# Block 1's first pair of token tiles: seven products in place of eight, in a linear-attention block gated by a mixer

## The chip, the core and the metric

One NeuronCore of a Trainium2 chip runs the whole kernel. The time is what the device needs for one execution, in microseconds (us); several executions are timed and their median is given. A profiled execution comes with a trace: for every instruction its engine, its start, its length and what it waited for. The engines are TensorE (PE, with the loading of its stationary operand shown apart as PEld), VectorE (DVE), ScalarE (ACT), GpSimd (POOL) and SyncE (SP), which issues most DMAs. POOL issues the DMAs that add to what lies at their destination.

## What is computed

2048 tokens of 512 features go through a layer norm, then two branches, whose product is added to the input:

```python
def _A_ref(x, wqkv, wo):                 # linear attention, 32 heads of 16
    q, k, v = ...                        # x @ wqkv, by heads
    phi = lambda t: jnp.where(t > 0, t + 1, jnp.exp(t)) + 1e-6
    pq, pk = phi(q), phi(k)
    kv = jnp.einsum("bhsd,bhse->bhde", pk, v)
    z = jnp.einsum("bhsd->bhd", pk)
    num = jnp.einsum("bhqd,bhde->bhqe", pq, kv)
    den = jnp.einsum("bhqd,bhd->bhq", pq, z)[..., None] + 1e-6
    return (num / den) ... @ wo
...
xn = _layernorm(x)
s = _A_ref(xn, A_wqkv, A_wo)
g = _silu(_B_ref(xn, B_w1, B_w2, B_w3, B_w4))
return x + s * g
```

`_B_ref` is a token mixer (shifts by one and two tokens between two 512 x 512 products) and a channel MLP of width 1376. For this change only the keys and queries matter: phi(x @ Wk) and phi(x @ Wq) for every token.

## The kernel before

**Tiling.** The tokens are cut into 16 tiles of 128, numbered 0 to 15, and four blocks of four tiles (block 1 is tiles 4 to 7). The 512 features are four chunks of 128. Every fp32 operand of a product is split into an upper half (rounded to the matmul format, by ScalarE) and a lower half (the rest, by VectorE's subtraction), and a product is three matmuls: upper x upper, upper x lower, lower x upper (`products`, L495). So a key tile, four chunks into 512 columns, is 12 matmuls (`project`, L707).

**Keys and queries one by one.** `key` (L783) and `query` (L806) make one tile each in one PSUM bank. In blocks 1 to 3 ScalarE copies the bank out with the token's scale (`zi`, `qi`). Then `phi_k` (L904) or `phi_q` (L915) applies phi: an exponential on ScalarE, a minimum and maximum on VectorE. For a key come two halves (`k4h`, `k4l` and so on) for the gram and a gather that adds it into `zacc`; for a query a store to memory (`pqd`).

**Keys and queries by pairs.** `pair_kq(i)` (L870) makes the keys and queries of tiles i and i+2 together. It sees them as a 2 x 2 block product, tokens (i, i+2) and feature halves against feature halves and (key, query), and forms the four results from seven products instead of eight, in Winograd's form of Strassen's method. A product covers two chunks, so it is six matmuls and a pair is 42, where four single results are 48. The products go into three banks: `pax`, `pbx`, which accumulates four of the seven with copies taken out between them, and `pex`. ScalarE copies four times (`p1x`, `p5x`, `u2x`, `zk`), VectorE joins three times (`zi`, `qi`, `qk`).

The seven products need sums of the weights (`kq_t1` to `kq_t4`, made once by `forms_w`, L820) and sums of tokens (`forms_x`, L844): eight additions on VectorE (`xf`), then four roundings on ScalarE and four lower halves on VectorE (`xs_0h`, `xs_0l` to `xs_3l`). The second argument `j0` of `forms_x` is the first pair of the block for which the sums are made: with 0 their width is 256 tokens (both pairs), with 1 it is 128 (the second pair alone).

Before the change, blocks 2 and 3 used `pair_kq` for both of their pairs. Block 1 made tiles 4 and 6 by `key` and `query` and only tiles 5 and 7 as a pair; its sums were made by `forms_x(1, 1)`. Block 0 uses single tiles throughout. [...]

**What a block's tokens wait for.** The transposed tokens are loaded (`xt`), and a gather adds each token's negative mean from a row in memory (`nrow`). That row comes from the tile statistics, by POOL, a small transpose on PE (`ab`), a copy (`ar`) and a store (`spread`, L631). ScalarE and VectorE then make the halves `u_0` to `u_3`, one per chunk (`load_u`, L660).

**Order.** The program is first written as a list of operations. `Plan.emit` (L285) then decides the order on each engine. It works through its own estimates of durations and picks, among operations whose inputs are there, the one that is due first. PE's due times follow the order of the list; those of the other engines are worked back from PE's. PE may run ahead of its list within a window of 9 us by these estimates, and free PSUM banks and pool tiles limit it. A table, `SOONER`, moves single operations: a pair (n, k) makes operation n due 0.25 k us earlier, or later for negative k. The order written into the program is fixed; on the chip only waits remain.

Of the kernel before, what the change touches and what calls it, by code (L numbers as in the profile page):

```python
# [411 lines left out]
def linear_attn_gated_by_mixer(  # L412
# [1224 lines left out]
    forms_x(1, 1)  # L1637
# [9 lines left out]
    for b in range(1, NQ):  # L1647
        t0 = b * QT
        if b > 1:
            pair_kq(t0)  # L1650
        else:
            for i in (t0, t0 + 2):
                key(i)
                query(i)
        if b > 1:
            gram(t0 - 3)
            gram(t0 - 1)
        if b < NQ - 1:
            for j in range(QT):
                load_rows(t0 + QT + j)  # L1660
            spread(b + 1)
            load_u(b + 1, 1)
            scale_x(t0 + QT, QT)
            forms_x(b + 1)
        if b == 3:
            sums_w4(1)
        pair_kq(t0 + 1)
        if b == NQ - 1:
            W1 = Weights("w1", w1)
            W1.split()  # L1670
        gram(t0)
        gram(t0 + 2)
        if b == 2:
            sums_w4(0)
        if b == 3:
            sums_w4(2)
# [37 lines left out]
    b = 2  # L1714
# [24 lines left out]
    b = 3  # L1739
# [29 lines left out]
    for b in range(NQ):  # L1769
# [35 lines left out]
        for j in range(QT):  # L1805
            i = b * QT + j
# [7 lines left out]
    for b in LINE:  # L1814
# [119 lines left out]
```

## Time and profile before

| | |
|---|---|
| median of three runs | 499.14 us (498.49 to 500.01) |
| profiled execution, its own time | 499.65 us |
| its span, first to last instruction | 497.9 us |
| granted TensorE clock | 1.00 |
| instructions | 9898, of them 3244 matmuls |
| DMA | 117.44 MB, mean 236 GB/s |
| POOL, busy | 121.5 us, 24% of the span |

In lines of the timeline stand the start (us from the span's start), the length (us), the engine, the line of the kernel, and the operation as output<-inputs; brackets hold how long the engine was idle before it and what ended that. Lines of a tile give a count and minimum, median and maximum in ns. Since most operations go through a few helpers, one line (L146 for matmuls, L168 for ScalarE, L191 and L201 for VectorE) stands for many; the tile's name tells them apart. Buffer numbers are left out of the names, so `xs_0l` stands for that sum in all blocks.

### The profile page before, as it was taken

To read this page: it belongs to the slowest core of one execution; us is meant where nothing else is said; L and a number is where in the kernel's file an instruction comes from. 1 tells how busy PE (TensorE), PEld (TensorE's weight loads), DVE (VectorE), ACT (ScalarE), POOL (GpSimd) and SP (SyncE) were. 2 spreads that over 40 slices of the span, in tenths; PEclk is the share of its full clock that TensorE was granted. 3 is DMA by queue.
4 is the path that set the end of the run, shared out by engine and by line. 5 is a ranking of instruction groups with operands and counts; after the bars stand their busy time and mean duration, and the time that the engine had idled before them with its cause. 6 is when DMAs were issued, how large, how long until landed. Compare 5 with 4: busy or idle time off the path is not lost.

```text
span 497.9 us, 9898 instructions
## 1 busy us (share of the span) xinstructions
PE 492.0 (99%) x3244; PEld 446.9 (90%) x3244; DVE 438.2 (88%) x874; ACT 373.9 (75%) x845; POOL 121.5 (24%) x214
## 2 busy tenths in 40 slices
PE   9999999999999999999999999999999999999996
PEld 6678877888888989899899999999999999999996
DVE  5898987789989759999999999999999789796964
ACT  5999999667787589999987667865686686655531
POOL 1384413357930223133100021100000000143420
PEclk9999999999999999999999999999999999999999
DMA  7869596999983899989986699884543799589996
GB/s 236 293 187 278 136 286 208 207 298 267 337 230 97 209 299 275 283 230 282 361 276 188 208 189 289 239 276 141 170 127 111 239 319 318 152 185 306 275 252 175
DMA packets 87083, 117.44 MB, mean 236 GB/s; under 512 B 10328, under 2 KB 39160, under 8 KB 87032
## 3 DMA queue, kind: packets, MB, share of 16 engines
q1 hardware_dynamic: 75512, 96.11, 59.2%
q0 software_dynamic: 11520, 20.71, 24.5%
q8 instruction: 25, 0.41, 0.3%
q14 instruction: 26, 0.21, 0.2%
HBM read 72.66 MB, written 39.93 MB: 226 GB/s over the span
## 4 chain that ended last, share of the span: by engine, by line
PE 62%; issue 4%; DMA 2%; ACT 1%; POOL 0%; DVE 0%; POOLq 0%; ACTq 0%
PE pb L146 11%; PE pbd L146 9%; PE acc L146 6%; PE pe L146 6%; PE ped L146 5%; PE pbs L146 5%; PE pbm L146 3%; PE pa L146 3%; PE pad L146 3%; PE pes L146 2%; DMA o<-xnd 2%; PE a L146 2%; PE h L146 2%; PE pem L146 2%; PE pas L146 1%
## 5 line engine op out<-in xcount | busy, mean ns | idle before, releaser
L225 POOL DMA_DIRECT2D xo<-x1d x12 | 11.2, 950 | 165.6 <-ACT d_s10h L168 111.1
L225 POOL DMA_DIRECT2D o<-xnd x16 | 14.0, 884 | 39.7 <-DVE o L191 24.9
L225 POOL DMA_DIRECT2D th<-in_x x14 | 12.3, 878 | 45.3 <-DVE th L201 13.0
L225 POOL DMA_DIRECT2D zacc<-ke x12 | 13.5, 1125 | 28.1 <-DVE u_2l L191 8.7
L168 ACT ACTIVATE th<-xo 128x512 f32<-128x512 f32 (+1 forms) x16 | 9.6, 612 | 13.6 <-DVE xo L201 9.8
L225 POOL DMA_DIRECT2D xt<-nrow x16 | 14.6, 1281 | 7.4 <-DVE kq_t31l L191 3.1
L191 DVE TENSOR_TENSOR ht<-h,abc 128x512 f32<-128x512 f32 x16 | 11.0, 687 | 5.0 <-PE h L146 4.9
L168 ACT ACTIVATE u<-pb 128x256 f32<-128x256 f32 x20 | 7.6, 382 | 7.4 <-PE pb L146 7.1
L196 POOL TENSOR_SCALAR w<-mv 128x4 f32<-128x4 f32 (+2 forms) x10 | 2.7, 269 | 41.2 <-ACT sq L168 40.9
L168 ACT ACTIVATE y<-o,nm,rs 128x512 f32<-128x512 f32 x16 | 12.0, 806 | 0.2 <-DVE wo_2l L191 0.2
L168 ACT ACTIVATE sq<-o,mv 128x512 f32<-128x512 f32 x16 | 11.4, 717 | 0.1
L201 DVE SCALAR_TENSOR_TENSOR pq<-pq,rd 128x512 f32<-128x512 f32 x16 | 10.8, 682 | 0.3
L201 DVE SCALAR_TENSOR_TENSOR qz<-pq,zb 128x512 f32<-128x512 f32 x16 | 10.9, 682 | 0.0
L168 ACT ACTIVATE p<-pe 128x256 f32<-128x256 f32 x20 | 7.7, 383 | 4.3 <-PE pe L146 3.7
L168 ACT ACTIVATE ht<-ht 128x512 f32<-128x512 f32 x16 | 9.9, 624 | 1.3 <-DVE ht L191 1.2
L1471 DVE TENSOR_REDUCE den<-qz 128x32 f32<-128x512 f32 x16 | 10.7, 677 | 0.1
L168 ACT ACTIVATE sq<-o 128x512 f32<-128x512 f32 x16 | 10.0, 623 | 1.0 <-DMA o<-xnd 1.0
L168 ACT ACTIVATE p<-pb 128x256 f32<-128x256 f32 x20 | 7.7, 384 | 3.6 <-PE pb L146 3.2
L613 POOL TENSOR_TENSOR rs<-w,nhalf 128x4 f32<-128x4 f32 (+2 forms) x10 | 9.4, 941 | 0.8
L201 DVE SCALAR_TENSOR_TENSOR th<-th,so 128x512 f32<-128x512 f32 x12 | 8.2, 682 | 1.1 <-ACT th L168 1.0
L168 ACT ACTIVATE x<-x,nm,rs 128x512 f32<-128x512 f32 x12 | 9.1, 802 | 0.0
L168 ACT ACTIVATE sq<-x,mv 128x512 f32<-128x512 f32 x12 | 8.6, 718 | 0.1
(2075 smaller groups left out, 2442.1 us busy)
## 6 DMA issues: line engine op xcount, KB each, us to landing
w_s<-in_w SPq DMA_DIRECT2D x28, 256.0 KB, 6.6
x<-in_x SPq DMA_DIRECT2D x16, 256.0 KB, 5.3
xt<-in_xt SPq DMA_DIRECT2D x16, 256.0 KB, 6.7
xnd<-x SPq DMA_DIRECT2D x16, 256.0 KB, 7.0
xt<-nrow POOLq DMA_DIRECT2D x16, 256.0 KB, 7.2
pqd<-qr SPq DMA_DIRECT2D x16, 256.0 KB, 5.6
o<-xnd POOLq DMA_DIRECT2D x16, 256.0 KB, 6.9
x1d<-o SPq DMA_DIRECT2D x16, 256.0 KB, 6.0
```

The source lines that it names most:

```text
L146: lambda: nc.tensor.matmul(out.get(), lhs.get(), rhs.get(), start=start, stop=stop, skip_group_check=more))
L168: nc.scalar.activation(out.get(), src.get(), func, scale=get(scale), **kw)
L191: self.vec(eng, out, [a, b], lambda: self.e(eng).tensor_tensor(out.get(), a.get(), b.get(), op=op), True)
L196: lambda: self.e(eng).tensor_scalar(out.get(), a.get(), get(s1), get(s2), **kw), False,
L201: lambda: self.nc.vector.scalar_tensor_tensor(out.get(), a.get(), get(s), b.get(), op0=op0, op1=op1),
L225: lambda: self.nc.gpsimd.dma_start(out.get(), get(src), accum_op=ALU.add), mb=mb)
L613: lambda: g.tensor_tensor(out.get(), src.get(), nh.get(), op=ALU.pow))
L1471: pl.add("DVE", .6, .68, [t], [den], lambda: nc.vector.tensor_reduce(den.get(), t.get().rearrange("p (h d) -> p h d", d=DH), axis=AX.X, op ...
```

## The change

`pair_kq` now makes block 1's first pair too (tiles 4 and 6), and the sums of block 1's tokens are made at double width, for both of its pairs. The table `SOONER` is another one: the list of operations is different from there on, so its numbers no longer mean the same operations, and it was searched again. Its entries reach over the whole kernel, so the order of any engine may differ anywhere.

```diff
     scale_x(QT, QT)
-    forms_x(1, 1)
+    forms_x(1, 0)
     spread(0)
...
     for b in range(1, NQ):
         t0 = b * QT
-        if b > 1:
-            pair_kq(t0)
-        else:
-            for i in (t0, t0 + 2):
-                key(i)
-                query(i)
+        pair_kq(t0)
         if b > 1:
             gram(t0 - 3)
...
     SOONER = (
-        48, -110, 56, 31, 58, 1, 65, 7, 88, -136, 91, -34, 100, 23, 101, 2, 106, -95, 119, 3, 121, -105, 124, 8,
...
+        21, 58, 25, 16, 26, -109, 34, 16, 37, 2, 42, 7, 48, 40, 65, 14, 74, 5, 79, -34, 82, -111, 88, -2, 91,
...
     )
```

127 rows, old and new, of the table SOONER are left out of this document.

## The prediction

> **What bounds the kernel now.** I read the page first: its busy times, then its chain of work that ended last.
>
> ```profile
> span 497.9 us, 9898 instructions
> PE 492.0 (99%) x3244; PEld 446.9 (90%) x3244; DVE 438.2 (88%) x874; ACT 373.9 (75%) x845; POOL 121.5 (24%) x214
> PE 62%; issue 4%; DMA 2%; ACT 1%; POOL 0%; DVE 0%; POOLq 0%; ACTq 0%
> ```
>
> TensorE is busy for all but 5.9 us of the span and carries most of the chain. Busy time alone would not prove it, so next comes the view of waits for PE (this is all of it).
>
> ```profile
> PE warm L146 <- POOL ones L529: 1.1, 1, 1.1
> PE g L146 <- ACT x0h L168: 0.6, 1, 0.6
> PE pem L146 <- ACT p5m L168: 0.3, 1, 0.3
> ```
>
> Three waits, 2.0 us together. A matmul taken away therefore shortens the run by its own pitch, as long as PE's next work is ready sooner by as much. Whether it is must be read in the stage that changes, which the timeline of PE places at 42 to 54 us. The view by windows, columns start:end, length, then busy us (x instructions) of PE, PEld, DVE, ACT, POOL, then PEclk:
>
> ```profile
> 19.00:42.00 23.00, 22.41 (x97) 17.47 (x97) 22.37 (x41) 22.69 (x48) 14.63 (x26) 1.00 0.72 207
> 42.00:54.00 12.00, 12.00 (x54) 9.74 (x53) 10.83 (x25) 11.53 (x27) 5.01 (x9) 1.00 0.89 256
> 54.00:68.00 14.00, 14.00 (x62) 11.16 (x61) 12.72 (x22) 13.96 (x26) 5.30 (x6) 1.00 0.74 153
> 68.00:83.00 15.00, 15.00 (x66) 12.00 (x66) 12.62 (x24) 14.31 (x33) 2.08 (x4) 1.00 0.95 327
> ```
>
> Over the span DVE and ACT look free (88% and 75%). Here they are nearly as full as PE. The change takes work from PE just where VectorE and ScalarE, which prepare PE's operands, are short of time. The whole prediction turns on that.
>
> **The matmuls removed.** PE's timeline, the edges of the stretch that the old form of tiles 4 and 6 fills, and the points where new inputs come in:
>
> ```profile
> 42.19 0.39 PE L146 MATMUL q<-wq_0h,u_0h 128*128 128x512 f32 x1
> 46.81 0.39 PE L146 MATMUL k<-wk_2h,u_2h 128*128 128x512 f32 x1
> 48.20 0.39 PE L146 MATMUL k<-wk_3h,u_3h 128*128 128x512 f32 x1
> 53.76 0.39 PE L146 MATMUL pbx<-wk_0h,u_0h 128*128 128x512 f32 x1
> 56.67 0.39 PE L146 MATMUL pex<-kq_t10h,xs_0h 128*128 128x512 f32 x1
> ```
>
> From 42.19 to 53.76 PE starts 50 matmuls: 48 of the pair (two tiles, a key and a query each, four chunks, three products of halves) and two of a gram. That is (53.76 - 42.19) / 50 = 0.2314 us apiece. Seven products take 7 x 2 chunks x 3 = 42 instead of 48. **Six fewer: 6 x 0.2314 = 1.39 us off PE.** The 0.39 us of a row is its length in the pipeline, not its price.
>
> [...]
>
> **The evacuations.** Each key and query was one ScalarE copy out of PSUM; the seven products need four such copies and three VectorE instructions. By tile (min/median/max ns):
>
> ```profile
> L168 ACT ACTIVATE zi<-k,rs x2: 682/686/689, 49.8 to 50.7; 128x512 f32<-128x512 f32 x2
> L168 ACT ACTIVATE p1x<-pbx,rs x5: 668/674/694, 57.0 to 116.9; 128x512 f32<-128x512 f32 x5
> L201 DVE SCALAR_TENSOR_TENSOR zi<-pax,rs,p1x x5: 737/744/749, 59.0 to 119.6; 128x512 f32<-128x512 f32 x5
> L201 DVE SCALAR_TENSOR_TENSOR qi<-pex,rs,u2x x5: 742/743/752, 64.3 to 125.1; 128x512 f32<-128x512 f32 x5
> L201 DVE SCALAR_TENSOR_TENSOR qk<-pbx,ns,p5x x5: 747/751/752, 63.7 to 127.3; 128x512 f32<-128x512 f32 x5
> ```
>
> ScalarE: four for four, no change. VectorE: three more, 0.744 + 0.743 + 0.751 = 2.24 us. What follows (exponential, minimum, halves) and the DMAs (a gather into zacc for each key, a store for each query) are the same four and four; nothing is moved past SP's or POOL's queue by the edit itself.
>
> **The sums of tokens.** They double in width, for both pairs at once. Block 1's are the narrow forms, block 2's and 3's the wide ones:
>
> ```profile
> L191 DVE TENSOR_TENSOR xf<-xf,xt x12: 284/417/426, 47.0 to 102.5; 128x256 f32<-128x256 f32 x8, 128x128 f32<-128x128 f32 x4
> L191 DVE TENSOR_TENSOR xs_0l<-xf,xs_0h x3: 418/683/684, 50.9 to 103.4; 128x512 fp32r<-128x512 f32 x2, 128x256 fp32r<-128x256 f32 x1
> L168 ACT ACTIVATE xs_0h<-xf x3: 407/613/619, 50.4 to 101.4; 128x512 fp32r<-128x512 f32 x2, 128x256 fp32r<-128x256 f32 x1
> ```
>
> Eight additions grow by 417 - 284 = 133 ns, four lower halves by 683 - 418 = 265 ns: 1.06 + 1.06 = 2.12 us of VectorE. Four upper halves grow by 613 - 407 = 206 ns: 0.82 us of ScalarE. In all **VectorE +4.36 us, ScalarE +0.82 us**. VectorE's busy time alone:
>
> ```profile
> 18.00:62.00 44.00, 42.15 (x80) 1.00 0.75 211
> 62.00:83.00 21.00, 17.38 (x32) 1.00 0.94 285
> ```
>
> It is free for 44.00 - 42.15 = 1.85 us up to 62 us, and for 3.62 us in the 21 us after. Of the 4.36 us, 2.51 must push something past 62 us. The cover is work nobody waits for soon: the last step of a query, which goes to a store only:
>
> ```profile
> 46.04 0.68 DVE L201 SCALAR_TENSOR_TENSOR qr<-qe,qi 128x512 f32<-128x512 f32 x1
> 52.23 0.69 DVE L201 SCALAR_TENSOR_TENSOR qr<-qe,qi 128x512 f32<-128x512 f32 x1
> 61.45 0.68 DVE L201 SCALAR_TENSOR_TENSOR qr<-qe,qi 128x512 f32<-128x512 f32 x1
> 62.06 0.68 DVE L191 TENSOR_TENSOR x5l<-x,x5h 128x512 fp32r<-128x512 f32 x1
> ```
>
> Those four are 2.73 us, just more than 2.51, so I cost VectorE's and ScalarE's additions at nothing on the path; without that cover it is the 2.51 us of the third rival.
>
> **What is late next.** The old form gave PE much to do before all its inputs were there. u_2 and u_3 are the last half of block 1's tokens:
>
> ```profile
> 45.43 0.69 DVE L191 TENSOR_TENSOR u_2l<-xt,u_2h 128x512 fp32r<-128x512 f32 x1 [1.01 <-ACT u_2h L168]
> 46.64 0.64 ACT L168 ACTIVATE u_3h<-xt 128x512 fp32r<-128x512 f32 x1 [0.20 <-DMA xt<-nrow]
> 50.88 0.42 DVE L191 TENSOR_TENSOR xs_0l<-xf,xs_0h 128x256 fp32r<-128x256 f32 x1
> 54.64 0.69 DVE L191 TENSOR_TENSOR kq_t10l<-kq_f,kq_t10h 128x512 fp32r<-128x512 f32 x1
> ```
>
> ScalarE stood 0.20 us for the DMA that centres u_3's tokens, so u_3's upper half cannot exist before 46.64 + 0.64 = 47.28. Before, PE had 24 matmuls on u_0 and u_1. Now it has 12: the two chunks of a11 x b11, of pair 4 and, taken forward, of pair 5. With the two of the gram that is 14 x 0.2314 = 3.24, so 45.43. u_2 gives 6 more (both pairs), to 46.82. Then PE stands for u_3: 47.28 - 46.82 = **0.46 us**. That is what I put on the path. It is 0 if block 1's DMAs land half a microsecond earlier, and 46.12 - 45.43 = 0.69 more if u_2l stays where it is; but u_2 was already there while ScalarE did other things (VectorE waited 1.01 us for ScalarE, and ScalarE for no DMA), so it can move.
>
> After u_3's six (to 48.67) the sums must be there. From u_3's landing, one addition, one rounding, one subtraction: 46.64 + 0.417 + 0.613 + 0.683 = 48.35, in time by 0.3. kq_t10l has to come forward from 54.64; its upper half was long done, so that is order only. From there one form feeds both pairs, 12 x 0.2314 = 2.78 us of PE, and costs VectorE two additions, the sum's lower half and two of a weight's: 2 x 0.417 + 3 x 0.683 = 2.88. So VectorE runs level with PE for some 8 us, with no reserve but grams 4 and 6. The added waits sit on VectorE: the three new instructions wait for PE, and everything behind them in VectorE's queue waits too.
>
> **Sum.** Against the profiled run (499.65 us, span 497.9): -1.39 + 0.46 = -0.93, so 498.72. That run lay 0.51 above the median of 499.14, so in medians **498.2**, -0.19%. Bounds: 0 and 1.15 (0.46 + 0.69) on the path give 497.75 to 498.9. The new order touches every stage, which I bound by half a microsecond either way: 497.3 to 499.4.
>
> About 0.3% (1.5 us; the three runs span 498.49 to 500.01) is what a measurement of this kernel can tell from no change. The line is 497.64.
>
> **Rivals.**
>
> *The order gives more than the products (C).* PE has one avoidable wait ahead of the stage, and a tail:
>
> ```profile
> 19.91 0.73 PE L146 MATMUL g<-k0h,x0h 128*128 128x512 f32 x2 [0.59 <-ACT x0h L168]
> 493.63 0.28 PE L146 MATMUL pbd<-w_l1h,dl1l 96*128 96x256 f32 x1
> 493.94 0.38 ACT L168 ACTIVATE th<-pbd 128x256 f32<-128x256 f32 x1 [1.14 <-PE pbd L146]
> ```
>
> If the new order starts the first gram without the 0.59 us and brings block 1's tokens in time, it is 499.14 - 1.39 - 0.59 = 497.2; a few tenths from the 4 us behind the last matmul would make it 496.6. Against it: 22.37 of 23 us of VectorE are taken there.
>
> *The gain is given back at block 2 (D).* Block 2's first tokens are just in time as well:
>
> ```profile
> 66.30 0.62 ACT L168 ACTIVATE u_0h<-xt 128x512 fp32r<-128x512 f32 x1
> 66.95 0.69 DVE L191 TENSOR_TENSOR u_0l<-xt,u_0h 128x512 fp32r<-128x512 f32 x1
> 68.07 0.40 PE L146 MATMUL pbx<-wk_0h,u_0h 128*128 128x512 f32 x1
> ```
>
> If they arrive as before and grams 4 and 6 have been spent filling the hole at 47 us, PE comes to 66.7 with u_0l not done before 67.64 and stands for what it saved: 499.1. The change then does nothing. For it: ScalarE had 13.96 of 14 us taken. Against it: PE's work for block 1's grams is movable.
>
> *VectorE becomes the bound (B).* If the urgent work cannot be put ahead, VectorE's 2.51 us fall on PE between 48 and 62 us: -1.39 + 2.51 = +1.1, with VectorE's own waits on PE (0.93 us before the old qk) +2.0: 500.3 to 501.2. It decides once the sums and t1 are not ready at 48.7.
>
> ```profile
> 63.67 0.75 DVE L201 SCALAR_TENSOR_TENSOR qk<-pbx,ns,p5x 128x512 f32<-128x512 f32 x1 [0.93 <-PE pbx L146]
> ```
>
> [...]
>
> **Numbers.** Forecast 0.43, of which 0.11 lies below 497.64; C 0.28; D 0.16; B 0.13. Faster 0.28 + 0.11 = 0.39; same 0.32 + 0.16 = 0.48; slower 0.13. Leaving out the lower part of C and the upper part of B, about 1 in 10 each, the range is 496.7 to 500.4.
>
> **What would show it.** 3238 matmuls instead of 3244; `pex` and `kq_t1` on PE at about 49 instead of 56.67; 24 `xf` additions of width 256, none of 128; VectorE's busy time near 442.5. Right: a PE idle of about half a microsecond at 47 us, put down to u_3. C: no idle there, and none at 19. D: PE idle or slipping at 67. B: several PE idles between 48 and 62 put down to xs or kq_t. A changed time from a stage after 150 us, which the edit does not touch, would make the reasoning wrong whatever the number.

## The result: slower, and the profile after

| | before | after |
|---|---|---|
| median | 498.97 us (498.49 to 500.01, 4 runs) | 503.73 us (502.86 to 504.45, 4 runs) |
| profiled execution | 499.65 us | 504.45 us |
| its span | 497.9 us | 502.7 us |

The ratio is 1.0094 [1.0083 to 1.0106]. The forecast was 498.2 us and its range ended at 500.4, so the prediction was wrong, and in sign. The page of the kernel after, its busy times and three of its rows by slices:

```profile
span 502.7 us, 9886 instructions
...
PE 494.0 (98%) x3238; PEld 444.7 (88%) x3238; DVE 442.1 (88%) x877; ACT 374.8 (75%) x845; POOL 127.4 (25%) x214
...
PE   8998999999999999999999999999999999999996
...
DVE  5998988788999868999999999999999899787954
...
PEclk9999999999999999999999999999999999999999
```

The amounts of work are as forecast: six matmuls fewer, and VectorE at 442.1 us (forecast 442.5). Yet PE's busy time rose by 2 us, and its row has an 8 in the fourth slice (37.7 to 50.3 us), where the edit sits. The first rows of the view of waits for PE in the kernel after:

```profile
PE pbx L146 <- DVE u_1l L191: 1.2, 1, 1.2
PE warm L146 <- POOL ones L529: 1.0, 1, 1.0
PE ab L151 <- POOL an L196: 0.6, 1, 0.6
PE k L146 <- ACT u_0h L168: 0.5, 1, 0.5
```

PE now waits for VectorE's lower half u_1l. PE's timeline there (kernel after):

```profile
44.58 0.39 PE L146 MATMUL pax<-wk_2l,u_2h 128*128 128x512 f32 x1
46.14 0.50 PE L146 MATMUL pbx<-wk_1h,u_1l 128*128 128x512 f32 x1 [1.18 <-DVE u_1l L191]
46.72 0.50 PE L146 MATMUL pex<-kq_t10h,xs_0h 128*128 128x512 f32 x1
47.06 0.40 PE L146 MATMUL pex<-kq_t10l,xs_0h 128*128 128x512 f32 x1
47.49 0.50 PE L146 MATMUL pbx<-kq_t20h,xs_1h 128*128 128x512 f32 x1
47.95 0.50 PE L146 MATMUL pex<-kq_t10h,xs_0l 128*128 128x512 f32 x1
48.29 0.57 PE L146 MATMUL pex<-kq_t11h,xs_0h 128*128 128x512 f32 x1
...
50.36 0.63 PE L146 MATMUL pax<-wk_3h,u_3l 128*128 128x512 f32 x1
50.78 0.63 PE L146 MATMUL pbx<-kq_t20l,xs_1h 128*128 128x512 f32 x1
51.21 0.63 PE L146 MATMUL pex<-kq_t11h,xs_0l 128*128 128x512 f32 x1
51.64 0.46 PE L146 MATMUL pbx<-wk_0h,u_0h 128*128 128x512 f32 x1
```

What four of these matmuls stood for, on VectorE and ScalarE (u_1l, at 45.41, is shown below):

```profile
46.06 0.62 ACT L168 ACTIVATE xs_0h<-xf 128x512 fp32r<-128x512 f32 x1
46.74 0.69 ACT L168 ACTIVATE p1x<-pbx,rs 128x512 f32<-128x512 f32 x1
47.21 0.69 DVE L191 TENSOR_TENSOR xs_0l<-xf,xs_0h 128x512 fp32r<-128x512 f32 x1
```

Two losses stand here. Up to 48.29 PE goes on as things are finished: at 46.14 for u_1l (VectorE, done at 46.10), at 46.72 for xs_0h (ScalarE, 46.68), at 47.49 for the bank that p1x empties (ScalarE, 47.43), at 47.95 for xs_0l (VectorE, 47.90). Six matmuls take 48.29 - 44.58 = 3.71 us where 6 x 0.232 = 1.39 would do, a loss of 2.32. Then eight matmuls take 51.64 - 48.29 = 3.35 us at twice the pitch (50.78 to 51.21 is 0.43), a loss of 1.49. The windows of PE (busy us, instructions, the granted clock, DMA share, GB/s) say why:

```profile
44.00:46.00 2.00, 0.96 (x5) 1.00 1.05 352
46.00:48.00 2.00, 1.75 (x5) 1.00 0.25 96
48.00:50.00 2.00, 2.00 (x6) 0.59 0.76 131
50.00:52.00 2.00, 2.00 (x7) 0.56 0.34 131
52.00:54.00 2.00, 2.00 (x10) 1.00 0.00 0
```

After the gap the clock was at half for some 3.4 us (0.50 from 49 to 51 us). Slow matmuls count as busy, and so does most of the time between matmuls that start late (46.14 to 48.29), which is why PE's busy time rose with six matmuls fewer.

To see all of the loss I add up PE's time beyond its ideal pitch: for each matmul, the time to the next one's start, less 0.232 us for 512 columns and 0.118 for 256, the median pitches in the trace of the kernel before (the few of 128 columns are put at 0.06, half of that). By stage, us, in the profiled runs:

```
                          0-20  20-40  40-60  60-180  180-end   sum
before                    7.58   0.24   0.03    0.30     8.40  16.55
after                     7.35   0.94   4.68    0.85     8.93  22.75
```

The excess grew by 6.20; less the six matmuls' 1.39 that is 4.81, against 504.45 - 499.65 = 4.80 measured. The stage from 40 to 60 us alone has 4.65 of it, 20 to 40 us 0.70, and the two stages after 60 us 1.08 together.

### The profile page after: what moved, and what is told of

The parts are those of the page before. It is cut to its first block, busy times and chain, and to the rows that moved or that the text cites. A ratio compares the mean times of both kernels' runs of the same rounds, so it can differ in the third digit from the quotient of the medians.

```text
span 502.7 us, 9886 instructions
## 1 busy us (share of the span) xinstructions
PE 494.0 (98%) x3238; PEld 444.7 (88%) x3238; DVE 442.1 (88%) x877; ACT 374.8 (75%) x845; POOL 127.4 (25%) x214
## 4 chain that ended last, share of the span: by engine, by line
PE 83%; DMA 6%; ACT 4%; DVE 3%; POOL 1%; issue 1%; SPq 1%; DVEq 0%; POOLq 0%
PE pb L146 11%; PE pbd L146 9%; PE h L146 7%; PE acc L146 6%; PE pe L146 6%; PE g L146 6%; PE pbx L146 5%; PE ped L146 5%; PE pbs L146 5%; PE pbm L146 4%; DMA xt<-nrow 4%; PE pa L146 3%; PE pex L146 3%; PE pad L146 3%; PE pes L146 2%; PE a L146 2%
## 5 line engine op out<-in xcount | busy, mean ns | idle before, releaser
L225 POOL DMA_DIRECT2D zacc<-ke x12 | 12.1, 1006 | 34.1 <-DVE u_2l L191 10.0
L196 POOL TENSOR_SCALAR w<-mv 128x4 f32<-128x4 f32 (+2 forms) x10 | 5.1, 507 | 43.2 <-ACT sq L168 42.9
```

The source lines that it names most:

```text
L196: lambda: self.e(eng).tensor_scalar(out.get(), a.get(), get(s1), get(s2), **kw), False,
L225: lambda: self.nc.gpsimd.dma_start(out.get(), get(src), accum_op=ALU.add), mb=mb)
```

## Experiments

Theories at the start: **1**, VectorE cannot make block 1's operands in time and PE starves between 44 and 60 us, worse where the clock then falls; **2**, the new order is worse all over; **3**, only u_1l's place in VectorE's queue is wrong. Times of the kernel before beside these runs were 498.89 to 499.09 us in median. The columns are those of the table above, then the run's median and ratio. The stages are those of one profiled execution, the median is of four to nine. (Two `qsum` matmuls with 0.3 us beyond the pitch each lie near 20 us, so the first column moves by up to 0.6 with the side on which they fall.)

```
                         20-40  40-60  60-180  180-end   median   ratio
after_again                1.46   2.61    0.47     8.97   502.64   1.0070 [1.0056, 1.0084]
fill_hole                  1.00   1.81    2.25     9.03   505.23   1.0131 [1.0115, 1.0147]
u1_before_sums             1.19   2.69    0.61     9.27   503.37   1.0088 [1.0075, 1.0102]
old_products_new_order     0.94   0.15    4.41    11.91   506.22   1.0151 [1.0132, 1.0170]
uncentred                  1.19   2.35    0.67     8.64   502.20   1.0066 [1.0054, 1.0078]
no_sums                    1.74   0.87    2.39     8.99   501.35   1.0055 [1.0037, 1.0073]
searched_after             1.26   2.48    2.83    17.27   512.36   1.0266 [1.0249, 1.0284]
searched_before            0.22   4.38    4.04    21.59   518.20   1.0379 [1.0343, 1.0415]
slack_after                6.41   4.14    0.97     9.16   508.55   1.0205 [1.0174, 1.0237]
slack_before               0.11   0.04    2.50    12.00   506.49   1.0162 [1.0129, 1.0196]
slack_block1               1.43   3.73    0.01     8.65   504.41   1.0108 [1.0095, 1.0121]
late_as_before             1.36   2.38    2.13    11.06   504.71   1.0117 [1.0087, 1.0147]
feed_block1                3.83   4.52    1.19    11.36   509.17   1.0147 [1.0093, 1.0202]
old_around_block1          2.64   1.20    2.56    10.84   505.31   1.0129 [1.0111, 1.0146]
before_loaded4             0.28   0.39    0.99    13.90   502.52   1.0056 [1.0035, 1.0077]
before_loaded7             0.22   2.58    0.87     9.54   505.68   1.0134 [1.0102, 1.0167]
before_loaded_late         0.24  -0.01    0.75     9.48   500.84   1.0044 [1.0027, 1.0062]
```

**The edit again**, with nothing changed.

> The changed kernel once more, for a second trace and its time beside the kernel before. Theory 1 (PE runs out of operands in block 1 between 44 and 60 us, and its clock falls to half after the gap): the gap before u_1l or the first sums is there again, 1 to 2 us long; the time is 4 to 5 us over before; where the clock does not fall, something else of 2 us must stand in its place. Theory 2 (the new order is worse all over): the 4.7 us are spread over stages, with under half of it between 40 and 60 us.

Its windows of PE:

```profile
44.00:46.00 2.00, 1.55 (x7) 1.00 1.06 320
46.00:48.00 2.00, 1.87 (x5) 1.00 0.52 199
48.00:50.00 2.00, 2.00 (x9) 1.00 0.76 131
```

The same matmul waits at the same place, but 0.5 us instead of 1.2, and the clock stays at 1.00. So how much the gap costs varies between executions. The half clock came with the longer gap here, but u1_before_sums below has a wait of 1.2 us at the same place and keeps its clock (0.999 over its profiled execution, where 3.35 us at half would leave 0.997), so the length of that wait alone doesn't decide it. The half clock isn't needed for the loss: 502.64 us is still 0.7% above before.

**Filling the hole, and u_1l first.** The first puts seven useless matmuls (1.62 us) ahead of the gap, their results left unread, to see whether the clock then stays up; the second holds every engine's order and only moves u_1l ahead of the two sums on VectorE that stood between a wait for tokens and it.

```diff
+            if op.order == 417:
...
+                for _ in range(FILL):
+                    self.nc.tensor.matmul(u.ap[:, :512], u_.ap[:, 2:2 + P], w_.ap[:, :512], start=True, stop=True)
```

```diff
-            ahead=6.0, table=SOONER)
+            ahead=6.0, table=SOONER, turns=TURNS)
```

`TURNS` lists all operations in the order in which they go; where an order is held or spliced below, this is the edit.

> The changed kernel with its order held, and seven more matmuls put on PE just behind the last one before the gap at 44.8 us; they write a bank that the next product overwrites, so they add 7 x 0.2314 = 1.62 us of work that nobody uses, in a gap of 1.9 us. If the half clock after the gap costs time (theory 1), no half-speed matmuls follow and the run is 1.5 to 2.5 us shorter than the changed kernel in spite of the added work. If the clock only hides waits for operands that would be there anyway, the time is the same within 0.5 us.

> The changed kernel with its order held but for one instruction: VectorE makes u_1l before the addition that waits for the last token DMA, not behind it. If the place in VectorE's queue is the cause (theory 3), PE loses the 1.2 us wait and the half clock behind it: 2 to 4 us faster than the changed kernel. If PE is out of operands anyway (theory 1), it goes on by one matmul and stands for the first sums instead, until about 46.5 us: 0 to 1 us faster.

With the hole filled, no such stretch at the half clock follows (the granted clock over the profiled execution is 0.998, and 3.35 us at half would leave 0.997), but the run isn't 1.5 to 2.5 us shorter: 505.23 us. In 40 to 60 us it loses 1.81 us besides the 1.62 of useless work, 3.43 together, against 4.68 with the half clock and 2.61 in the edit's other profile; behind the filling PE stands again, at 47.68, until p1x has emptied a bank. The rest lies elsewhere, 1.1 us of it in a wait for u_2h at 74 us, in block 2. So the filling doesn't tell what the half clock costs the run.

The second run speaks against theory 3. In its view of waits for PE

```profile
PE pex L146 <- ACT xs_0h L168: 1.2, 1, 1.2
```

the gap has passed from u_1l to the first sum. What goes ahead on VectorE pushes something else that PE needs.

**Old products under the new table.** The kernel before with the new table's entries carried over to its list (666 of 675 have a counterpart).

```diff
-    forms_x(1, 0)
+    forms_x(1, 1)
...
-        pair_kq(t0)
+        if b > 1:
+            pair_kq(t0)
+        else:
+            for i in (t0, t0 + 2):
+                key(i)
+                query(i)
```

> The kernel before, with single keys and queries for tiles 4 and 6 and narrow sums, but with the entries of the new order table carried over to the same operations (666 of 675). Theory 2 (the order is at fault): 2 to 5 us slower than before. Theory 1 (the edit takes PE's stock of work that needs no sums): no gap between 44 and 60 us, and within 1.5 us of before, since what else the new order costs is small.

Block 1 has no gap then: 0.15 us beyond the pitch. So under these entries the gap at 40 to 60 us goes with the products. The time, 506.22 us, is above what either theory gave: the table makes holes of its own elsewhere in this kernel (4.0 us around 100 us). Since it was made for another list, theory 2 isn't weighed by that.

**Searched orders.** Both kernels got tables searched for longer, in the first two for the best fit to the planner's own estimates, in the next three with random extra time on GpSimd's operations, DMAs and evacuations.

```diff
     SOONER = (
-        21, 58, 25, 16, 26, -109, 34, 16, 37, 2, 42, 7, 48, 40, 65, 14, 74, 5, 79, -34, 82, -111, 88, -2, 91,
...
```

> The edit, with a table of turns that was searched longer and over all stages. Theory 1 (in block 1 the sums come out of VectorE too late for any order, since VectorE has 4.4 us more to do by 62 us): TensorE still runs out of operands between 40 and 60 us, its time beyond the ideal pitch there is 1.5 us or more, and the kernel stays above the kernel before, at 500 us or more. Theory 2 (the edit is fine and the table that came with it serves it badly, in block 1 and in the later stages): less than 0.5 us beyond the pitch in 40 to 60 us, no wait of TensorE over 0.5 us after 25 us, and the time is below the kernel before, at about 497 us (ratio 0.994 to 0.998).

> The kernel before, its table of turns searched as long as that of the edit above: the fair partner for it. Theory 2: a longer search gains something here too, about 1 us, and the edit searched stays below it by about its six matmuls, 1.39 us. Theory 1: this kernel is the fastest of the four, by 1.5 us or more.

> The edit, with a table of turns for the first half of the kernel that was searched with random extra time on every GpSimd operation, DMA and evacuation, so that the order keeps slack against them. Theory A (orders that fit a plan exactly break on the chip, since GpSimd's small operations and the DMAs take other times than planned; the edit itself is sound): no wait of TensorE over 0.7 us between 25 and 110 us, less than 1 us beyond the pitch in 40 to 60 us, and a time below that of the edit by 2 us or more, 498 to 500.5 us. Theory B (the edit's sums starve TensorE in block 1 whatever the order): 1.5 us or more beyond the pitch stays in 40 to 60 us, and the time stays above 501 us.

> The kernel before, with a table searched in the same way over the whole kernel: the partner of the run above. Theory A: it gains too, to 495 to 498 us; the edit beside it costs or gains no more than 2 us. Theory B: it is at least 3 us below the edit searched in the same way.

> The edit, with a table in which only the turns of the first 1200 operations (up to about block 1) were searched so, the others as the edit has them. Theory A: the excess in 40 to 60 us falls to about 1 us, the stages after 180 us stay as in the edit (about 7 us beyond the pitch after 180 us), and the time falls by 1 to 2.5 us, to 500 to 501.5 us. Theory B: 502 to 503.5 us.

No run came to the time that theory 2 or A gave. By the letter, searched_after fits theory 1 and slack_after theory B, but every order found so is slower on the chip than the one it replaced, by up to 19 us, the unchanged kernel's too, so their times don't speak for the edit's sums as the cause. PE has single waits of up to 3.9 us. Two rows of GpSimd and three of VectorE in slack_after belong to that wait:

```profile
24.57 1.03 POOL L613 TENSOR_TENSOR an<-pu,nhalf 128x4 f32<-128x4 f32 x1
...
27.54 4.20 POOL L613 TENSOR_TENSOR an<-pu,nhalf 128x4 f32<-128x4 f32 x1
```

```profile
27.78 0.69 DVE L201 SCALAR_TENSOR_TENSOR kr<-kt,kr 128x512 f32<-128x512 f32 x1
...
30.19 0.69 DVE L191 TENSOR_TENSOR kq_f<-wk_s,wq_s 128x512 f32<-128x512 f32 x1
30.79 0.74 DVE L201 SCALAR_TENSOR_TENSOR kt<-wneg,mv,k 128x512 f32<-128x512 f32 x1
```

The same operation took 1.03 us and then 4.20, while VectorE ran five instructions with two SBUF operands without a break from 27.78 to 30.79; it ended 31.74 - 30.79 = 0.95 us after the first one that reads PSUM (`k`) had begun. The rows show the two at the same time, not that one held up the other. PE paid for the long one: its `ab` waited 3.9 us for `an`.

So "searched anew" is worth nothing by itself, and the searched runs don't decide between theories 1 and 2 by their times. By their stages they say this: the three orders of the edit have 2.48 to 4.14 us in 40 to 60 us, while slack_before has 0.04. (searched_before has 4.38, most of it one wait of 2.5 us for u_0h that ends at 44.5, with matmuls 0.43 us apart, as at the half clock above, for 3.4 us behind it; so an order can spoil that stage for the old products too.)

**What the operands wait for.** The edit's order held, and block 1's gather of the mean left out; and, separately, block 1's sums left out, the products reading the tokens' own halves instead.

```diff
-                if centred:
+                if centred and b != 1:
```

```diff
-        for c in range(h):
+        for c in range(h if b != 1 else 0):
...
-        for n, v in enumerate(t):
+        if b == 1:
+            for n in range(4):
+                f[f"s{n + 1}"] = lambda c, j, n=n: ut(b, n % 2 * h + c, 2 + j * P, 2 + (j + 1) * P)
+        for n, v in enumerate(t if b != 1 else ()):
```

> The edit's order of all instructions held as it was; block 1's subtraction of the mean row from its tokens, a DMA that gathers into the tokens, is left out, so that nothing of block 1 waits for it. If the gap at 44 to 46 us comes of the sum on VectorE that waits 0.85 us for this DMA, ahead of u_1l in the queue, the gap shrinks to about 0.3 us and the excess of 40 to 60 us to 1 us or less; the kernel comes to about 500.5 us. If the gap is VectorE's load alone, it stays at 0.6 to 1.2 us and the time at 502 to 503.5 us.

> The edit's order held; block 1's sums of tokens (eight operations on VectorE, with the rounding of the sums) are left out, and the seven products read the tokens' own two halves in their place. Theory 1 (VectorE's load of sums starves TensorE): the gap at 44 to 46 us closes, the excess of 40 to 60 us falls under 0.6 us, and the time falls by 2 us or more against the edit, to 500 to 501 us. If the gap has another cause (the halves u of the tokens themselves come late from ScalarE and VectorE), it stays above 1.5 us.

VectorE's timeline in the kernel after, and with the gather left out:

```profile
44.60 0.43 DVE L191 TENSOR_TENSOR xf<-xt,xt 128x256 f32<-128x256 f32 x1 [0.85 <-DMA xt<-nrow]
45.06 0.42 DVE L191 TENSOR_TENSOR xf<-xf,xt 128x256 f32<-128x256 f32 x1
45.41 0.69 DVE L191 TENSOR_TENSOR u_1l<-xt,u_1h 128x512 fp32r<-128x512 f32 x1
```

```profile
43.95 0.42 DVE L191 TENSOR_TENSOR xf<-xt,xt 128x256 f32<-128x256 f32 x1
44.40 0.43 DVE L191 TENSOR_TENSOR xf<-xf,xt 128x256 f32<-128x256 f32 x1
44.74 0.69 DVE L191 TENSOR_TENSOR u_1l<-xt,u_1h 128x512 fp32r<-128x512 f32 x1
```

Without the gather the wait of 0.85 us is gone and u_1l comes 0.67 us sooner, but 2.35 us stay in 40 to 60 us, against 2.61 and 4.68 in the two profiles of the edit: the DMA sets how long the first gap is, not that PE starves. Without the sums 0.87 us is left, a little more than the 0.6 expected; 0.54 of it is the gap at 47.57, where PE stands for the bank that p1x empties, so it comes of the product form and not of a sum. The rest of the stage is as theory 1 has it. The time, 501.35 us, fell by 1.3 us against after_again, less than the 2 expected. The profiled execution was the slowest of the six (503.84) and has 1.74 us in 20 to 40 us and a wait of 1.3 us for p1x at 121 us. Leaving out the sums takes four roundings from ScalarE too, so this run doesn't part the two engines.

**Spliced orders.** The edit with the late order of the kernel before; with 20 to 66 us rearranged besides; and with the order of before up to 34 us and from 100 us on. The edit of the code is `TURNS` again.

> The edit with its own order up to 100 us, and from there the order of the kernel before. If the loss sits between 20 and 62 us, the later stages give back no more than 0.5 us: 502.0 to 503.0 us, with 2.3 us or more beyond the pitch in 40 to 60 us. If the new order of the later stages carries it, the time falls to 500.5 us or less.

> As the run before it, with the order of the stretch from 20 to 66 us rearranged for tokens that land late (random delays of up to 2.5 us on each transfer). If an order can feed TensorE in block 1, less than 1 us beyond the pitch is left in 40 to 60 us and the time is 498 to 500 us. If the products wait for late tokens and eight sums whatever the order, 2.3 us or more stay there, and the time is 501 us or more.

> The edit with the order of the kernel before up to 34 us and from 100 us on; only the stretch between, with block 1's new products and sums, is arranged anew. If the loss in 20 to 40 us is one of order and that in 40 to 60 us one of the products' operands, the first goes (0.4 us or less beyond the pitch in 20 to 40 us) and the second stays (2 us or more), and the time is 500 to 501.5 us. If both are of order, the time comes to 498.5 us or less. If both stay, it is 502.5 us or more.

Late_as_before gave nothing back, and lost 2 us more after 180 us than the edit, so its time doesn't tell where the loss is; feed_block1 has more in 20 to 60 us, and its six executions fall into two groups (509.0 to 509.4 and 502.0 us). Old_around_block1 has the least of the edit's orders in 40 to 60 us, 1.20 us: there six more matmuls that need only u_0 and u_1 (of tiles 5 and 7) stand ahead of the sums, and behind 47.1 us PE runs on. But it has 2.64 in 20 to 40, where PE waits 1.4 us for k2l, a lower half that VectorE makes for a gram, and 0.6 us at 45.3 for u_0h. From 20 to 60 us together the complete kernels with the edit have 3.7 us or more (fill_hole, whose useless matmuls count as work, aside); without the gather it is 3.5, without the sums 2.6, and the kernel before has 0.3. New holes after 60 us make the three times say little.

**VectorE's load alone.** The last runs leave products and order of the kernel before, and only add useless additions on VectorE: seven (4.2 us) or four (2.4 us) in block 1, or seven some 40 us later.

```diff
     forms_x(1, 1)
+    junk = piece('junk')
+    for _ in range(7):
+        pl.tt(junk, XT[1, 0], XT[1, 0], ALU.add)
```

> The kernel before in its own order, with 7 useless additions of 512 columns on VectorE (4.2 us) among block 1's token operations at 42 to 46 us. Theory V (VectorE has no slack there; its load alone makes the loss): TensorE idles 2 us or more beyond the pitch in 40 to 60 us, against 0.01 in the kernel before, and the time rises by 2 to 4 us, to 501 to 503 us. Theory O (VectorE's load is covered, as the prediction had it, and the orders alone lose the time): under 0.6 us beyond the pitch, and 498.5 to 500 us.

> The same with 4 additions (2.4 us). The prediction's cover, four deferrable operations of 2.73 us, would hide them whole. Theory V: part shows, 0.5 to 2 us, 499.5 to 501 us. Theory O: nothing shows, 498.5 to 499.5 us.

> The same 7 additions at 79 to 84 us (four) and 92 to 94 us (three), where VectorE idles 2.4 and 1.9 us of 4. Both theories: within 0.8 us of the kernel before, 498.5 to 499.8 us; more would say that any work added to VectorE costs, wherever it stands.

PE's windows with seven, with four, and with seven later:

```profile
44.00:48.00 4.00, 3.71 (x17) 1.00 1.06 341
48.00:52.00 4.00, 2.56 (x12) 1.00 0.74 221
```

```profile
44.00:48.00 4.00, 4.00 (x19) 1.00 1.07 309
48.00:52.00 4.00, 4.00 (x19) 1.00 0.88 300
```

```profile
44.00:48.00 4.00, 4.00 (x19) 1.00 1.07 331
48.00:52.00 4.00, 4.00 (x19) 1.00 0.91 273
```

And the wait behind it, with seven:

```profile
PE k L146 <- DVE u_3l L191: 1.4, 1, 1.4
```

```profile
48.57 0.68 DVE L201 SCALAR_TENSOR_TENSOR qr<-qe,qi 128x512 f32<-128x512 f32 x1
49.70 0.69 DVE L191 TENSOR_TENSOR u_3l<-xt,u_3h 128x512 fp32r<-128x512 f32 x1
```

By the stage this is theory V of the expectations: 4.2 us of VectorE work in block 1, in the kernel before and its own order, costs PE 2.58 us there, and the same work 40 us later costs nothing there. Four additions cost 0.39 us, less than expected. The order is held, so a query's last step (48.57) stays ahead of u_3l: the runs show what the load costs, not whether moving such work behind would have covered it.

The times of all three lie higher than that (even the control is 1.9 us above before): each has a new wait of 0.6 to 2.4 us for `p1d` near 470 us, which the kernel before has not and the three spliced runs with its late order have too; its cause is open. Against the control, seven cost 505.68 - 500.84 = 4.8 us in median and four 1.7. The two profiled executions, 503.09 and 500.71 us, differ by 2.4, about what the stage shows; the slower executions were not profiled.

## Why the prediction was wrong

- **The matmuls removed**: right, 3238, and the 1.39 us are in the account above.
- **Evacuations and sums, VectorE +4.36 us**: right in amount, 442.1 - 438.2 = 3.9 us over the span.
- **"I cost VectorE's and ScalarE's additions at nothing on the path"**: this step failed. Its sum was 4.36 us less 1.85 free, covered by four deferrable instructions of 2.73. The dose shows where that breaks: 2.4 us of load are nearly free (0.39), 4.2 us cost 2.58. The 1.85 us were hardly room for sums: 1.01 us of them is a wait for u_2h, made of just those tokens, and 0.44 one for PE. The cover was too small even by its own lines: x5l starts at 62.06 us, so that moving it frees nothing before 62, and it is an operand of a gram, not a query's last step. And it stood in the wrong place: the qr of 52.23 and 61.45 lie behind the point where PE was waiting. In the kernel after, VectorE runs no qr at all between 40.1 and 56.3 us, and PE starves all the same. Adding up free time over 44 us did not ask whether it came before the deadline. ScalarE's part isn't shown apart: it made xs_0h and p1x, for which PE stood too, but only after VectorE's sum and u_1l.
- **"What is late next", 0.46 us for u_3**: wrong in place and size. u_1l was late, not u_3: done at 43.33 + 0.69 = 44.02 before and at 45.41 + 0.69 = 46.10 after, since five of the eight sums and a wait for tokens went ahead of it on VectorE; u_3's upper half was there at 44.53 + 0.63 = 45.16, two microseconds sooner than the sum had it. The 12 matmuls on u_0 and u_1 that the sum counts on weren't there either: the order left the six of tiles 5 and 7 to 51.64 us and later (old_around_block1 takes them forward). In place of 0.46 us the stage lost 4.65 us in the profiled run, and 2.6 in another execution. VectorE's row of u_1l in the kernel before:

```profile
43.33 0.69 DVE L191 TENSOR_TENSOR u_1l<-xt,u_1h 128x512 fp32r<-128x512 f32 x1
```

- **"VectorE runs level with PE for some 8 us"**: I had seen that there was no reserve, and gave it no price. PE's matmuls from 46 to 48.3 us start 0.3 to 0.6 us apart, as operands and a bank come free.
- **Rival B** had the mechanism, VectorE as the bound. Its price, 500.3 to 501.2 us, was below the median by 2.5 to 3.4 us. Of this, 1.49 is the half clock in one of the profiles; the tokens' wait (0.85 us on VectorE) and 0.7 us in 20 to 40 us, where PE waits 0.6 us for `an` from GpSimd, which it doesn't in the kernel before, are further parts that it left out. Its chance of 0.13 was the larger error. Its sign in the profile was half right: idles between 44 and 60 us, but put down to u_1l first.
- **"Order ±0.5"**: too narrow. Orders of one and the same kernel differed by up to 19 us here. That no order of the edit can beat the kernel before isn't shown, only that none of the eight tried did, and none of the runs gave a version faster than the kernel before.

## What to carry to other kernels

Where one engine is the bound and another prepares its operands, price an edit in the stage where it lands, and by deadlines: free time of the preparing engine counts only if it lies before the operand is due and isn't itself a wait for the same data. Here, taking work from a full engine and giving it to one that stands just ahead of it in the chain moved the bound, although that engine had 12% free over the span. And orders searched against estimates lost more on the chip here than the edit that they served could bring.

## What the chip showed besides

- After a stretch of 3.7 us in which PE ran six matmuls with gaps of up to 1.3 us, the granted clock fell to half (0.50 from 49 to 51 us) for 3.35 us, with matmuls 0.43 us apart. With a wait of 0.5 us at that place, in the next run of the same kernel, it did not (1.00 from 44 to 52 us), nor in u1_before_sums with one of 1.2 us (0.999 over the profiled execution). What decides it isn't shown.
- In slack_after above, a GpSimd operation on 128x4 elements took 4.20 us, and for 3.0 us of it VectorE ran two-operand instructions without a break. That these hold GpSimd up isn't shown: in the kernel after, two such operations (`an`, at 27.29 and 29.27 us) took 1.19 and 1.10 us while VectorE ran seven two-operand instructions from 27.71 to 32.02 us without a break. A long operation stands in feed_block1 too, where one took 3.87 us and the least of its four 0.22:

```profile
L196 POOL TENSOR_SCALAR an<-mv x4: 218/332/3868, 28.6 to 84.1; 128x4 f32<-128x4 f32 x4
```

The gather of block 1's tokens stood behind it on GpSimd and issued at 37.58 us instead of 34.01 in the kernel after, and VectorE waited for it:

```profile
45.50 0.43 DVE L191 TENSOR_TENSOR xf<-xt,xt 128x256 f32<-128x256 f32 x1 [3.46 <-DMA xt<-nrow]
...
50.41 0.42 DVE L191 TENSOR_TENSOR xf<-xt,xt 128x256 f32<-128x256 f32 x1 [2.22 <-DMA xt<-nrow]
```
